# Round-robin PSUM banks for a fast-matrix-product MLP, and attention sums in four column tiles

## The chip, the cores and the metric

One core of a Trainium2 chip. The metric is device time in microseconds (us) of one execution. Ratios are the mean time of one kernel's fast runs over that of the other's fast runs of the same rounds, so they are not quite the ratio of the medians quoted beside them; brackets hold their 95% interval.

TensorE multiplies matrices; VectorE, ScalarE and GpSimd work element by element. A *bank* is one PSUM tile of 128 x 512 fp32, in which a product is summed; the program lets the next product into it only when the readers of the last one are through. A *column tile* is a matmul that uses 64 or 32 of TensorE's 128 columns (a *row tile*, 64 of its rows), so that several can be in flight; the *mode* is how TensorE is divided. In a timeline, brackets at the end of a line hold the engine's idle time before it and what ended it.

## The reference

```python
q, k, v: (8, 12, 448, 64)            # batch, heads, sequence, head_dim, fp32
q_n, k_n = rmsnorm(q, g_q), rmsnorm(k, g_k)
attn = softmax(q_n @ k_n.T / sqrt(64))
x = (attn @ v) as (8*448, 12*64)     # bridge
h = x @ w_in                         # (3584, 768) @ (768, 2048)
out = (h - tanh(h)) @ w_out          # (3584, 2048) @ (2048, 768)
```

## The kernel before: the parts concerned

TensorE runs two streams, interleaved by hand. *Attention* goes in 48 steps, one per batch and pair of heads (six to a batch): scores transposed (keys on partitions), `exp` on ScalarE, sums over keys as a product with ones, values. *MLP* of batch b-1 runs between the pieces of attention of batch b; `run(gap)` issues a quarter of a step's share of it. From batch 1 on, both MLP layers use a seven-product scheme for 2 x 2 blocks: a *set* is seven products, several of which accumulate in the same PSUM bank, and readers combine them.

```python
ORDER = (1, 5, 6, 2, 7, 3, 4)
ps_s = pool("ps_s", bufs=4, space=PSUM)     # attention: four banks
ps_m = pool("ps_m", bufs=1, space=PSUM)     # MLP: "ma", "mc" once, "mb" twice
...
def totals(s, dn):                          # sums over keys: two column tiles of 64
    ...
    nc.tensor.matmul(dn[h * D : (h + 1) * D, :S], lhsT=ones[:CP, :D], rhs=p[:, h, :], ...)
    rd = sp.tile([P, S], F32, name="rd")
    nc.vector.reciprocal(rd, dn[:, :S])
...
def slot(s):                                # one step of attention
    scores(s + 1, 0); load(s + 2, "v")
    run(gap)
    norm(s + 3)                             # GpSimd: squares and a power; VectorE: sums
    rd = totals(s, sc_bank()); divide(s, values(s, sc_bank()), rd)
    run(gap)
    scores(s + 1, 1); add(s + 1)            # VectorE adds four tiles of exponentials to one
    run(gap)
    turn(s + 2, sc_bank(), sc_bank())       # transposes
    norm_q(s + 3); load(s + 4, "kq")
    run(gap)
```

(`has(...)` guards and the loop over products are cut.) After product 3 of a set `shrink` (tanh on ScalarE, a subtraction on GpSimd) and then `factors` (VectorE: a difference that needs that subtraction) are put off to the end of the next product.

## Time and profile before

| | |
|---|---|
| time | 1589.95 us median of 4 (1588.75 to 1591.17) |
| TensorE / VectorE / ScalarE / GpSimd busy | 94 / 50 / 28 / 39% |
| a normal step in steady state | 29.85 us |
| one step in each batch | 31.76 us |

The last two rows come from the starts of the transposes in the trace. The long step looks like this in the timeline of the kernel before (start, length, engine, line, operation):

```profile
995.32 2.43 PE L448 MATMUL ma<-xT,w_f 128*128 128x224 f32 x12
995.36 3.17 DVE L376 TENSOR_TENSOR sum<-sum,p 112x896 f32<-112x896 f32 x2 [1.19 <-ACT p L362]
998.44 0.62 DVE L530 TENSOR_TENSOR s<-mb,s 128x448 f32<-128x448 f32 x1
999.11 1.78 PE L448 MATMUL mb<-xT,w_f 128*128 128x224 f32 x8 [1.36 <-DVE s L530]
```

VectorE adds exponentials until 998.5; only then does it read product 6 out of bank `mb` (L530), and product 7, which accumulates in that bank, starts 1.36 us late.

### The profile page before, as it was taken

What the parts mean: (1) busy time and instruction counts of PE and PEld (TensorE: products, weight loads), DVE (VectorE), ACT (ScalarE), POOL (GpSimd) and SP (SyncE); (2) the same over time, 40 slices, a digit from 0 to 9 for tenths busy, and PEclk for the clock granted to TensorE, in tenths of its full rate; (3) what the DMA queues carried; (4) which work ended last, traced back from release to release, by engine and by line L of the source; (5) the groups of instructions that cost most, each with busy time, mean ns of one, the idle gap of its engine ahead of it and who ended that gap; (6) DMA issues with size and microseconds to landing.
All of it is one profiled execution on the core that took longest, in us unless ns stands there. A gap on an engine that the chain in (4) does not pass through costs nothing.

```text
span 1588.6 us, 19983 instructions
## 1 busy us (share of the span) xinstructions
PE 1494.3 (94%) x7440; PEld 1164.7 (73%) x7440; DVE 788.6 (50%) x1004; ACT 446.4 (28%) x870; POOL 624.4 (39%) x516
## 2 busy tenths in 40 slices
PE   3988768998999999999999999999999999999997
PEld 1336456446878878878877887787877887789997
DVE  6788558865454345434544445434544344522211
ACT  4554234512322223222331232321331232210210
POOL 6655446552452234422453235423444234311410
PEclk9999879999999999999999999999999999999999
DMA  7554575577545554555554564465454664455564
GB/s 193 177 181 165 195 256 166 138 196 229 164 141 161 147 151 144 152 166 148 154 170 123 158 177 131 147 184 139 137 167 133 171 166 137 135 152 162 174 196 105
DMA packets 253983, 257.80 MB, mean 162 GB/s; under 512 B 143413, under 2 KB 198709, under 8 KB 253877
## 3 DMA queue, kind: packets, MB, share of 16 engines
q1 hardware_dynamic: 253552, 256.43, 55.4%
q8 instruction: 61, 1.00, 0.3%
q14 instruction: 46, 0.37, 0.1%
q10 hardware_dynamic: 324, 0.00, 0.0%
HBM read 223.35 MB, written 33.03 MB: 161 GB/s over the span
## 4 chain that ended last, share of the span: by engine, by line
PE 74%; DVE 13%; POOL 3%; DMA 3%; issue 2%; ACT 2%; SPq 2%; ACTq 0%; DVEq 0%; POOLq 0%
PE mb L448 24%; PE ma L448 16%; PE mc L448 15%; PE sc L357 8%; PE sc L383 6%; DVE rd L400 2%; DVE w_out L79 2%; PE sc L395 2%; POOL sq L310 2%; DVE sum L376 2%; DMA w_f<-w_in 1%; PE mb L616 1%; DVE rr L311 1%; ACT p L362 1%; DVE w_out L82 1%
## 5 line engine op out<-in xcount | busy, mean ns | idle before, releaser
L362 ACT ACTIVATE p<-sc,rr 112x448 f32<-112x448 f32 x384 | 212.5, 638 | 224.0 <-PE sc L357 162.0
L448 PE MATMUL mb<-tt,w_f 128*128 128x224 f32 x768 | 166.5, 361 | 17.3 <-DMA w_f<-w_in 16.3
L357 PE MATMUL sc<-qT,kT 64*112 64x448 f32 x768 | 179.5, 574 | 2.2 <-DVE rd L400 1.5
L448 PE MATMUL ma<-xT,w_f 128*128 128x224 f32 x768 | 163.8, 365 | 11.9 <-DMA w_f<-w_in 11.9
L448 PEld LDWEIGHTS mb<-tt,w_f 128*128 128x128 f32 x768 | 142.6, 192 | 42.6 <-issue 22.8
L448 PEld LDWEIGHTS ma<-xT,w_f 128*128 128x128 f32 x768 | 149.7, 197 | 18.7 <-issue 6.2
L315 POOL TENSOR_TENSOR rr<-rr,neg_half 112x16 f32<-112x16 f32 (+1 forms) x49 | 140.7, 2871 | 51.3 <-DVE rr L314 50.3
L400 DVE RECIPROCAL rd<-sc 128x448 f32<-128x448 f32 x42 | 124.0, 2953 | 34.9 <-PE sc L395 34.0
L448 PE MATMUL ma<-gT,w_f 128*128 128x224 f32 x672 | 139.2, 356 | 0.0
L448 PEld LDWEIGHTS ma<-gT,w_f 128*128 128x128 f32 x672 | 125.3, 190 | 15.3 <-issue 15.3
L448 PE MATMUL mb<-tg,w_f 128*128 128x224 f32 x672 | 135.1, 354 | 0.0
L383 PE MATMUL sc<-p,v_nat 112*64 112x448 f32 x672 | 133.4, 539 | 0.0
L448 PEld LDWEIGHTS mb<-tg,w_f 128*128 128x128 f32 x672 | 126.2, 190 | 7.3 <-issue 7.3
L376 DVE TENSOR_TENSOR sum<-sum,p 112x896 f32<-112x896 f32 x80 | 95.8, 1198 | 58.2 <-ACT p L362 52.6
L357 PEld LDWEIGHTS sc<-qT,kT 64*112 64x112 f32 x768 | 65.9, 176 | 79.4 <-issue 62.1
L535 POOL TENSOR_TENSOR u<-u,s 128x448 f32<-128x448 f32 x32 | 36.5, 1141 | 221.0 <-DVE u L534 194.7
L311 DVE TENSOR_REDUCE rr<-sq 112x8 f32<-112x512 f32 x96 | 65.4, 681 | 113.9 <-POOL sq L310 113.9
L310 POOL TENSOR_TENSOR sq<-q_nat 112x512 f32<-112x512 f32 x48 | 50.0, 1041 | 150.5 <-DVE rr L311 103.2
L383 PEld LDWEIGHTS sc<-p,v_nat 112*64 112x64 f32 x672 | 48.3, 137 | 78.0 <-issue 78.0
L448 PE MATMUL mb<-xT,w_f 128*128 128x224 f32 x384 | 87.4, 366 | 17.2 <-DVE s L530 11.4
L504 POOL TENSOR_TENSOR gT<-s,th 128x448 f32<-128x448 f32 x64 | 75.0, 1172 | 62.1 <-ACT th L503 62.1
L448 PEld LDWEIGHTS mb<-xT,w_f 128*128 128x128 f32 x384 | 71.3, 194 | 34.6 <-issue 20.4
(108 smaller groups left out, 2146.0 us busy)
## 6 DMA issues: line engine op xcount, KB each, us to landing
w_f<-w_in SPq DMA_DIRECT2D x224, 384.0 KB, 3.6
w_f<-w_out SPq DMA_DIRECT2D x147, 512.0 KB, 4.3
w_raw<-in_moe_w_out_dram SPq DMA_DIRECT2D x32, 384.0 KB, 3.4
k_nat<-in_k_dram SPq DMA_DIRECT2D x96, 112.0 KB, 3.3
q_nat<-in_q_dram SPq DMA_DIRECT2D x48, 224.0 KB, 3.7
v_nat<-in_v_dram SPq DMA_DIRECT2D x48, 224.0 KB, 4.7
w_in<-w_out SPq DMA_DIRECT2D x28, 384.0 KB, 5.6
out_dram<-th SPq DMA_DIRECT2D x192, 56.0 KB, 2.7
```

The costliest lines, as they stand in the source:

```text
L79: nc.vector.tensor_scalar(out=bits, in0=bits, scalar1=4, scalar2=1, op0=ALU.logical_shift_left, op1=ALU.logical_shift_right)
L310: nc.gpsimd.tensor_tensor(out=sq, in0=rows, in1=rows, op=ALU.mult)
L311: nc.vector.reduce_sum(rr[:, "kq".index(name)], sq, axis=AX.X)
L315: nc.gpsimd.tensor_tensor(out=r, in0=r, in1=neg_half[:, : r.shape[1]], op=ALU.pow)
L357: nc.tensor.matmul(sc[:CP, :S], lhsT=kT[r, c * CP : (c + 1) * CP], rhs=qT[r, :], start=True, stop=True)
L362: nc.scalar.activation(p[:, h, i, :], tiles[h][:CP, :S], AF.Exp, scale=rr[:, 0, 2 * c + h : 2 * c + h + 1])
L376: nc.vector.tensor_tensor(out=t, in0=t, in1=part, op=ALU.add)
L383: nc.tensor.matmul(av[h * D : (h + 1) * D, :S], lhsT=v_nat[:, h, c, :], rhs=p[:, h, c % 2, :], start=(c == 0), stop=(c == NCH - 1),)
L400: nc.vector.reciprocal(rd, dn[:, :S])
L448: nc.tensor.matmul(bank[:, f * HS : (f + 1) * HS], lhsT=w[:, f * depth + c, :], rhs=moving[p](c), start=(first and f == 0 and c == 0), sto ...
L504: eng.tensor_tensor(out=g[:, rows, cols], in0=h, in1=th, op=ALU.subtract)
L535: nc.gpsimd.tensor_tensor(out=u3, in0=u3, in1=s5, op=ALU.add)
```

## The change

Its intent: give every MLP bank more time between two products, halve TensorE's time for the sums over keys, and leave MLP's tiling mode twice in a step rather than three times.

```diff
-    ORDER = (1, 5, 6, 2, 7, 3, 4)
+    ORDER = (1, 5, 6, 2, 3, 7, 4)
-    ps_s = pool("ps_s", bufs=4, space=PSUM)
-    ps_m = pool("ps_m", bufs=1, space=PSUM)
+    ps_s = pool("ps_s", bufs=5, space=PSUM)
+    ps_m = pool("ps_m", bufs=3, space=PSUM)
...
+            for p in ORDER:
+                first = p not in (2, 3, 7)
+                bank = banks[p] = mm_bank() if first else banks[{2: 1, 3: 5, 7: 6}[p]]
...                                       # readers of products 5 and 7 (layer 1; layer 2 likewise)
-                    nc.scalar.copy(out=s5, in_=v)
+                    nc.vector.tensor_tensor(out=s5, in0=v, in1=s1, op=ALU.add)
...
-                    nc.vector.tensor_tensor(out=u3, in0=v, in1=s1, op=ALU.add)
-                    nc.gpsimd.tensor_tensor(out=u3, in0=u3, in1=s5, op=ALU.add)
+                    nc.vector.tensor_tensor(out=u3, in0=v, in1=s5, op=ALU.add)
+                    nc.vector.tensor_tensor(out=s1, in0=v, in1=s1, op=ALU.add)
...
+    def totals_by_halves(s, dn):         # four column tiles: 2 heads x 2 halves of the queries
+        ...
+                    r = (2 * h + n) * BL
+                    nc.tensor.matmul(dn[r : r + BL, :HS], lhsT=ones[:CP, :BL],
+                                     rhs=p[:, h, n * HS : (n + 1) * HS], ...)
+        nc.vector.reciprocal(rs, dn[:, :HS])
...                                       # rows_out: 4 rows to DRAM; rows_in: back to 128 partitions
+    def late_slot(s):                    # from batch 2 on, in place of slot
+        totals_by_halves(s, sc_bank()); scores(s + 1, 0); load(s + 2, "v")
+        run(gap / 2)
+        rows_out(s); norm(s + 3)
+        run(gap / 2)
+        rows_in(s); turn(s + 2, sc_bank(), sc_bank()); load(s + 4, "kq")
+        run(gap)
+        divide(s, values(s, sc_bank())); scores(s + 1, 1); add(s + 1)
+        run(gap)
+        norm_q(s + 3)
+        run(gap)
```

(Cut: guards, layer 2, and the rest of `factors`, which is split by product.)

More of the change, by code (lines that the diff above doesn't have):

```diff
@@ L143, in bounded_path, with mm_bank @@
     wp = wp_stack.enter_context(tc.tile_pool(name="wp", bufs=1))
-    ps_s = pool("ps_s", bufs=4, space=PSUM)
-    ps_m = pool("ps_m", bufs=1, space=PSUM)
-    def mm_bank(tag):
-        return ps_m.tile([P, 512], F32, name=tag, bufs=2 if tag == "mb" else 1)
+    ps_s = pool("ps_s", bufs=5, space=PSUM)
+    ps_m = pool("ps_m", bufs=3, space=PSUM)
+    def mm_bank():
+        return ps_m.tile([P, 512], F32, name="mm")
     loaded = {}
@@ L298, in ring_load @@
                 nc.sync.dma_start(out=t, in_=w_out_dram[:, BLOCKS[p], j].rearrange("p f d -> p (f d)"))
-    normed, turned, probs, sums, xT, tt = {}, {}, {}, {}, {}, {}
+    normed, turned, probs, sums, whole, xT, tt = {}, {}, {}, {}, {}, {}, {}
     def norm(s):
@@ L398, in totals, with rows_out, rows_in, divide @@
                 )
-        rd = sp.tile([P, S], F32, name="rd")
+        rd = whole[s] = sp.tile([P, S], F32, name="rd")
         nc.vector.reciprocal(rd, dn[:, :S])
-        return rd
-    def divide(s, av, rd):
+    def totals_by_halves(s, dn):
+        t = sums.pop(s)
+        parts = t if t else [probs[s, c // 2][:, :, c % 2, :] for c in range(NCH)]
+        for i, p in enumerate(parts):
+            for h in range(2):
+                for n in range(2):
+                    r = (2 * h + n) * BL
+                    nc.tensor.matmul(
+                        dn[r : r + BL, :HS], lhsT=ones[:CP, :BL], rhs=p[:, h, n * HS : (n + 1) * HS],
+                        start=(i == 0), stop=(i == len(parts) - 1),
+                    )
+        rs = whole[s] = sp.tile([P, HS], F32, name="rs")
+        nc.vector.reciprocal(rs, dn[:, :HS])
+    def rows_out(s):
+        rs = whole[s]
+        row = whole[s] = scratch.tile([2, S], F32, name="row", bufs=2)
+        nc.sync.dma_start(
+            out=row.rearrange("h (n q) -> (h n) q", n=2), in_=rs.rearrange("(g i) q -> g i q", i=BL)[:, 0, :]
+        )
+    def rows_in(s):
+        row = whole[s]
+        rd = whole[s] = sp.tile([P, S], F32, name="rd")
+        nc.sync.dma_start(
+            out=rd,
+            in_=bass.AP(tensor=row.tensor, offset=row.offset, ap=[[S, 2], [0, D], [1, S]]),
+        )
+    def divide(s, av):
         b, hp = steps[s]
+        rd = whole.pop(s)
         x = xT[b, hp] = xp.tile([P, S], F32, name="xT")
@@ L439, in products @@
         took = 4 * HS / ENGINE_NS
+        banks = {}
         def product(j, p, bank, first):
@@ L458, in product @@
                 fn()
-        pending = None
         for j in range(count):
             use = done_with(j)
-            ma, mc = mm_bank("ma"), mm_bank("mc")
-            yield from product(j, 1, ma, True)
-            use(1, ma)
-            yield took
-            if pending:
-                yield from pending()
-            yield from product(j, 5, mc, True)
-            use(5, mc)
-            yield took
-            mb = mm_bank("mb")
-            yield from product(j, 6, mb, True)
-            use(6, mb)
-            yield took
-            for p, bank in ((2, ma), (7, mb), (3, mc)):
-                yield from product(j, p, bank, False)
+            for p in ORDER:
+                first = p not in (2, 3, 7)
+                bank = banks[p] = mm_bank() if first else banks[{2: 1, 3: 5, 7: 6}[p]]
+                yield from product(j, p, bank, first)
                 use(p, bank)
                 yield took
-            def pending(j=j, mb=mb, use=use):
-                yield from product(j, 4, mb, False)
-                use(4, mb)
-                yield took
-        yield from pending()
     def hidden(b):
@@ L508, in done_with, with factors @@
             s1, s2, s5, u3 = part("s1"), part("s2"), part("s5"), part("u3")
-            def factors(first):
+            def factors(p):
                 if b == 0:
@@ L515, in factors @@
                 f1, f2, f4 = (t2[:, i, up] for i in range(3))
-                if first:
+                if p == 3:
                     nc.vector.tensor_tensor(out=f1, in0=g12, in1=g11, op=ALU.subtract)
+                elif p == 7:
                     nc.vector.tensor_tensor(out=f2, in0=g22, in1=f1, op=ALU.subtract)
@@ L533, in use, with rest @@
                 elif p == 7:
-                    nc.vector.tensor_tensor(out=u3, in0=v, in1=s1, op=ALU.add)
-                    nc.gpsimd.tensor_tensor(out=u3, in0=u3, in1=s5, op=ALU.add)
-                    late["todo"].append(lambda: shrink(down, high, u3, nc.gpsimd))
+                    nc.vector.tensor_tensor(out=u3, in0=v, in1=s5, op=ALU.add)
+                    nc.vector.tensor_tensor(out=s1, in0=v, in1=s1, op=ALU.add)
+                    def rest():
+                        shrink(down, high, u3, nc.gpsimd)
+                        factors(7)
+                    late["todo"].append(rest)
                 elif p == 3:
@@ L541, in rest @@
                         shrink(up, high, s2, nc.gpsimd)
-                        factors(True)
+                        factors(3)
                     late["todo"].append(rest)
@@ L549, in rest @@
                         shrink(down, low, s1, nc.gpsimd)
-                        factors(False)
+                        factors(4)
                     late["todo"].append(rest)
@@ L584, in use @@
                 elif p == 5:
-                    nc.scalar.copy(out=s5[:, low], in_=v)
+                    nc.vector.tensor_tensor(out=s5[:, low], in0=v, in1=s1[:, low], op=ALU.add)
                 elif p == 6:
@@ L590, in use @@
                 elif p == 7:
-                    nc.vector.tensor_tensor(out=y2[:, high], in0=v, in1=s1[:, low], op=ALU.add)
-                    nc.gpsimd.tensor_tensor(out=y2[:, high], in0=y2[:, high], in1=s5[:, low], op=ALU.add)
+                    nc.vector.tensor_tensor(out=y2[:, high], in0=v, in1=s5[:, low], op=ALU.add)
+                    nc.vector.tensor_tensor(out=s1[:, low], in0=v, in1=s1[:, low], op=ALU.add)
                 elif p == 3:
@@ L611, in project_first @@
         for n in range(CD):
-            bank = mm_bank("mb")
+            bank = mm_bank()
             for f in range(CF):
@@ L667, in first_slot @@
         if has(s + 2):
-            turn(s + 2, mm_bank("mb"), mm_bank("mb"))
+            turn(s + 2, mm_bank(), sc_bank())
         load(s + 4, "kq")
@@ L674, in first_slot @@
         if has(s):
-            rd = totals(s, mm_bank("mc"))
+            totals(s, mm_bank())
         if has(s + 2):
@@ L682, in first_slot @@
         if has(s):
-            divide(s, values(s, mm_bank("ma" if s < NP - 1 else "mb")), rd)
+            divide(s, values(s, mm_bank()))
         if has(s + 3):
@@ L696, in slot @@
             norm(s + 3)
-        rd = totals(s, sc_bank())
-        divide(s, values(s, sc_bank()), rd)
+        totals(s, sc_bank())
+        divide(s, values(s, sc_bank()))
         run(gap)
@@ L710, in slot @@
         run(gap)
+    def late_slot(s):
+        gap = gap_ns(s)
+        totals_by_halves(s, sc_bank())
+        if has(s + 1):
+            scores(s + 1, 0)
+        if has(s + 2):
+            load(s + 2, "v")
+        run(gap / 2)
+        rows_out(s)
+        if has(s + 3):
+            norm(s + 3)
+        run(gap / 2)
+        rows_in(s)
+        if has(s + 2):
+            turn(s + 2, sc_bank(), sc_bank())
+        if has(s + 4):
+            load(s + 4, "kq")
+        run(gap)
+        divide(s, values(s, sc_bank()))
+        if has(s + 1):
+            scores(s + 1, 1)
+            add(s + 1)
+        run(gap)
+        if has(s + 3):
+            norm_q(s + 3)
+        run(gap)
     load(0, "kq")
@@ L718, in bounded_path @@
     for s in range(NP, NS):
-        slot(s)
+        slot(s) if s < 2 * NP else late_slot(s)
     run(1e9)
```

## The prediction

> **What bounds the kernel now.** I read the page first (busy shares, slices, clock), then the table of windows by stage, then the waits of TensorE, then the timeline of one attention step, which is the unit that repeats.
>
> The page says that TensorE is busy for nearly the whole span at full clock, and that the idle part lies in the first quarter:
>
> ```profile
> PE 1494.3 (94%) x7440; PEld 1164.7 (73%) x7440; DVE 788.6 (50%) x1004; ACT 446.4 (28%) x870; POOL 624.4 (39%) x516
> ...
> PE   3988768998999999999999999999999999999997
> ...
> PEclk9999879999999999999999999999999999999999
> ...
> L448 PE MATMUL mb<-tt,w_f 128*128 128x224 f32 x768 | 166.5, 361 | 17.3 <-DMA w_f<-w_in 16.3
> ...
> L395 PE MATMUL sc<-sum,ones 112*64 112x448 f32 x160 | 38.9, 565 | 0.0
> ```
>
> Three windows, chosen by stage (weights still being converted; steady; MLP alone), give the same in numbers:
>
> ```profile
> 115.00:265.00 150.00, 113.83 (x515) 85.32 (x512) 106.91 (x148) 59.14 (x120) 73.91 (x58) 0.87 0.62 202
> 409.00:1406.00 997.00, 988.88 (x5149) 802.76 (x5148) 455.37 (x547) 266.91 (x514) 376.11 (x314) 1.00 0.52 152
> 1433.00:1580.00 147.00, 147.00 (x777) 144.25 (x776) 32.18 (x53) 17.18 (x35) 33.32 (x31) 1.00 0.58 166
> ```
>
> The columns are the window, its length, then PE, PEld, DVE, ACT and POOL busy, clock, DMA share and GB/s. In the middle 997 us TensorE is idle for 8.1 us and VectorE busy for under half: TensorE's own work sets the time there, and only fewer TensorE cycles or the removal of those 8.1 us can shorten it. From 115 to 265 us it is idle for 36 us; another chain sets the time there.
>
> The waits of TensorE over the whole run name both kinds of idleness:
>
> ```profile
> PE mb L337 <- DVE n L321: 25.9, 6, 7.6
> PE mb L448 <- DMA w_f<-w_in: 22.1, 3, 11.0
> PE ma L448 <- DMA w_f<-w_in: 11.9, 4, 4.6
> PE mb L448 <- DVE s L530: 11.4, 7, 3.3
> ```
>
> The first lies before 115 us (the first queries are normalised late), the next two are weight blocks that come late in batch 0, and the fourth is the one that recurs: 8.1 us of it are six waits of 1.36 us, one per batch, and 3.3 us one wait in batch 0.
>
> One attention step in steady state, TensorE alone (start, length, then the group):
>
> ```profile
> 915.43 1.76 PE L357 MATMUL sc<-qT,kT 64*112 64x448 f32 x8
> 917.12 2.54 PE L448 MATMUL ma<-xT,w_f 128*128 128x224 f32 x12
> 919.50 2.43 PE L448 MATMUL mc<-tt,w_f 128*128 128x224 f32 x12
> 921.77 0.92 PE L448 MATMUL mb<-tt,w_f 128*128 128x224 f32 x4
> 922.62 0.97 PE L395 MATMUL sc<-sum,ones 112*64 112x448 f32 x4
> 923.42 3.18 PE L383 MATMUL sc<-p,v_nat 112*64 112x448 f32 x16
> 926.53 1.78 PE L448 MATMUL mb<-tt,w_f 128*128 128x224 f32 x8
> ```
>
> Lengths overlap, so I take starts. One matmul of the program is two records. From 919.50 to 921.77 twelve MLP records take 2.27 us, 189 ns each. The sums over keys (L395) hold TensorE from 922.62 to 923.42, 0.80 us for two head halves side by side. Read instruction by instruction, two such records start 6 to 8 ns apart and the next two 376 ns later (448 columns), except the first round, 426 ns. From one start of L395 (922.62) to the next (952.47) a step is 29.85 us; one step in each batch is 31.76.
>
> **What the Trainium skill says.** "TensorEngine Tiling (Array Packing)", section Key Properties: changing the tiling mode drains TensorE, and tiles run independently. The trace agrees: the last MLP record before the sums starts 283 ns ahead of them where 189 is normal (+94), the first round costs another 50, and the way back costs 95 and 104 more.
>
> "TensorE: Matmul & The Clock Gate", section Part 3: Packing small matmuls, gives a pack's span as one matmul plus about 4 ns for each further tile. The 6 to 8 ns between the two tiles here agree; that four column tiles in fp32 do the same, no trace here shows yet.
>
> The same page, section Architectural detail, calls ScalarE and VectorE strict FIFO. The recurring wait is this: the add that frees a product's bank (L530) stands behind the sums of attention, which wait for exponentials, and came at 998.44 for a product finished about a microsecond earlier.
>
> "DMA: Bandwidth & Descriptors", Anatomy of one DMA, gives a fixed cost of about 2.0 us plus bytes over 436 GB/s. This trace lands 56 KB in 2.7 us and 224 KB in 3.7 to 4.7 us, so the same size of cost.
>
> **The change part by part.**
>
> 1. *Sums over keys in four column tiles, from batch 2 on (36 of 48 steps).* Four tiles of 32 columns by 224 queries replace two of 64 by 448. A round of 224 fp32 columns should take half of 376, 188 ns, and there are still two rounds: 752 becomes 376 ns, if the four tiles really run at once. Saved: 0.376 us a step.
>
> 2. *Fewer trips away from MLP mode.* Before, a step has three trips into a tiled mode: scores, sums with values, scores. Measured over the steady stage as the time from the last MLP start before to the second after, less two times 189 ns: scores 1.889 us against 4 x 0.376 = 1.504 pure, so 0.385 of switching; sums and values 4.107 against 3.760, so 0.347. In all 2 x 0.385 + 0.347 = 1.117 us. After, there are two: sums with scores, values with scores. Each has an entry (0.144), an exit (0.200) and an inner change, which batch 0's prologue shows for values to scores as 94 + 91 = 0.185 us. That is 2 x 0.529 = 1.058. Saved: 0.059. Parts 1 and 2: 0.43 us a step, x 36 = 15.5 us. The transposes move but run in MLP's mode.
>
> 3. *MLP banks go round.* Before, product 7 accumulates on 6's bank with only product 2 between, so 6's reader has one product (2.27 us) before TensorE waits. After, in order 1, 5, 6, 2, 3, 7, 4, every second product on a bank, and every reuse of a bank, has two products between (4.5 us). L530's delay of 1.36 us fits in. The step that holds it is 1.9 us long over the normal one (31.76 - 29.85; scores stretched by a late bank are in it, and attention's fifth bank should end them). Saved: 6 x 1.9 = 11.4 us steady, and 3.3 us in batch 0.
>
> 4. *Readers of the banks.* Product 5's copy (ACT, 521 ns) becomes a VectorE add, product 7 gets a second VectorE add, and GpSimd's add (1141 ns) goes. VectorE gets 2 x 0.62 us more in each of four sets and 2 x 0.39 in each of three projections: 7.3 us a batch. Against it the reciprocal (2953 ns for 448 columns) works on 224, by proportion 1.48 us: six steps give 8.9 us back. VectorE stays at half busy, off the path.
>
> 5. *Rows through DRAM.* The reciprocals go out as 4 rows and come back to 128 partitions (229 KB). From the steps above: sums end at about T+0.6 us, reciprocal T+2.3, out issued then and landed near T+5, back near T+9. The multiplication that needs it follows values at about T+17 (sums and scores 2.4, two MLP gaps of 5.2, transposes 0.8, values 3.1). So hidden, with 8 us to spare. The load adds 36 x 0.23 = 8 MB to 257.
>
> 6. *Batch 0.* Product 4 now runs before the next set's product 1, so one weight block is fetched ahead of the seven writes that keep a set in DRAM. In the before trace block 6 of the second set waited 10.98 us behind these. I expect TensorE to have one product (2.3 us) more done when it stalls, but VectorE's conversion now also stands behind product 5, which ACT served before. Net 1 us saved, give or take 5.
>
> Sum: 15.5 + 11.4 + 3.3 + 1 = 31 us. I take off 4 us for new waits: the multiplication, then the sums' adds, now come in one burst after values, and VectorE is blocked there for about 5 us. So 1590.4 - 27 = 1563 us.
>
> **The rivals.**
>
> A. *Four tiles don't overlap, or pay per instruction.* Sixteen matmul and weight records fall in 0.38 us, 24 ns each; the transposes here issue eight in 0.385 us, 48 ns each, but those are bound by their 112 columns. If 48 ns were the limit, the sums would take 0.8 us again and part 1 would give nothing: 1576. The queue running ahead of TensorE speaks against it.
>
> B. *The wait moves.* The burst on VectorE delays some other reader by more than two products, or sums at the head of a step wait for the adds. The adds should end about 8 us after values start and the sums come 15 us after: little room for it. If once per batch 1.5 us come back: 1572.
>
> C. *Broadcast late.* If the DMA queue stands still for over 8 us, values' multiplication waits; TensorE would feel it only through the fifth bank. In 36 steps of 1 us: 1595 or more. The steady queue keeps five blocks ahead, which speaks against it.
>
> D. *Batch 0 gains more.* The 36 us idle there is latency in a loop, and taking GpSimd's add out of it could give 5 to 10 us: 1555.
>
> **Range and chances.** The steady part is well determined (15 and 11 us, each give or take 3), batch 0 is not (give or take 5), and new waits can only cost. 8 in 10: 1552 to 1577. The 2% line is 1558.6, half a standard deviation below my figure: faster 0.30, within 2% 0.69, slower 0.01.
>
> **What would show it.** The step in steady state 29.4 us, all six of a batch alike; sums from first start to the scores' start about 0.53 us with the mode change (0.42 without); no wait of TensorE for the product 6 add; the reciprocal at 1.5 us; the broadcast landed before values end; idle from 115 to 265 us still near 30 us. I am wrong if four tiles start more than 20 ns apart, if a step still stays at 29.8, if a new VectorE or DMA wait of TensorE over 5 us in sum appears after 400 us, or if batch 0 moves by more than 6 us.

## The result, and the profile after

1572.99 us, median of 4 (1571.13 to 1575.12), against 1589.95: ratio 0.9894 [0.9877, 0.9911], within 2% and inside the range, 10 us above the figure. From the page and from a table of windows of the changed kernel:

```profile
PE 1474.9 (94%) x7584; PEld 1159.5 (74%) x7584; DVE 771.3 (49%) x1110; ACT 424.8 (27%) x817; POOL 615.0 (39%) x463
```

```profile
115.00:265.00 150.00, 117.84 (x520) 88.00 (x520) 107.52 (x159) 59.02 (x120) 71.69 (x57) 0.89 0.64 209
400.00:1390.00 990.00, 980.37 (x5316) 805.68 (x5315) 437.29 (x628) 253.74 (x480) 379.91 (x276) 1.00 0.56 161
```

TensorE is still the bound, with 32 us idle in the early window and 9.6 us in the steady one (36 and 8.1 before). The steady idle time is not gone. From 400 to 1400 us it has one new name (total, times, longest):

```profile
PE mm L481 <- issue: 9.6, 6, 1.6
```

One step of the changed kernel, TensorE alone:

```profile
933.27 0.59 PE L411 MATMUL sc<-sum,ones 112*32 112x224 f32 x8
933.78 1.76 PE L358 MATMUL sc<-qT,kT 64*112 64x448 f32 x8
...
940.88 0.55 PE L334 MATMUL sc<-ident,k_nat 112*128 112x112 f32 x4
...
947.05 3.23 PE L384 MATMUL sc<-p,v_nat 112*64 112x448 f32 x16
950.21 1.76 PE L358 MATMUL sc<-qT,kT 64*112 64x448 f32 x8
```

The sums hold TensorE from 933.27 to 933.78, 0.51 us with the mode change that follows (0.80 before, where values follow in the same mode). Read one by one, the four tiles start 6 to 8 ns apart and the second round 214 ns after the first: they do run at once. A normal step is 29.42 us, 0.43 less than before.

But one step in each batch takes 31.52 us. Here it is, one stretch on TensorE, VectorE, ScalarE and GpSimd:

```profile
966.67 0.58 ACT L517 ACTIVATE th<-s 128x448 f32<-128x448 f32 x1 [0.22 <-DVE s L558]
967.25 1.04 POOL L311 TENSOR_TENSOR sq<-q_nat 112x512 f32<-112x512 f32 x1 [9.33 <-DVE rr L312]
...
968.03 2.43 PE L481 MATMUL mm<-tt,w_f 128*128 128x224 f32 x12
...
969.30 2.90 POOL L316 TENSOR_TENSOR rr<-rr,neg_half 112x16 f32<-112x16 f32 x1 [1.01 <-DVE rr L315]
...
971.07 2.45 PE L481 MATMUL mm<-xT,w_f 128*128 128x224 f32 x12
972.16 1.13 POOL L518 TENSOR_TENSOR gT<-s,th 128x448 f32<-128x448 f32 x1
...
973.33 0.62 DVE L531 TENSOR_TENSOR tg<-gT 128x448 f32<-128x448 f32 x1 [4.11 <-POOL gT L518]
973.87 0.62 DVE L549 TENSOR_TENSOR u<-mm,s 128x448 f32<-128x448 f32 x1
974.41 0.62 DVE L550 TENSOR_TENSOR s<-mm,s 128x448 f32<-128x448 f32 x1
...
975.12 1.19 PE L481 MATMUL mm<-tt,w_f 128*128 128x224 f32 x5 [1.61 <-issue]
```

Read it backwards. TensorE wants the bank of product 7 for the next set's product 5. Product 7's two adds (L549, L550) end at 975.02; the product itself was done at about 968.2, just after product 4 began to run (968.03). They stand behind L531, a difference that needs GpSimd's subtraction L518, and L518 stands behind the normalisation's power L316, 2.90 us. The column says "issue", so the profile shows nothing that TensorE waited for; that it was this bank is read from the VectorE rows (the adds end 0.10 us before product 5 starts), and late_factors and four_four test it. Start by start, product 5 makes 1.85 us of the long step's 2.10; the other 0.26 falls on product 6, which starts at 977.62 when product 4's add, behind the same queue, has left its bank (977.57).

Where the 19.4 us between the two profiled runs (1588.6 and 1569.2) went, by milestones of the MLP stream in the traces:

| stretch | before | after | difference |
|---|---|---|---|
| start to batch 0's MLP | 120.4 | 119.2 | -1.2 |
| batch 0's MLP | 245.9 | 240.3 | -5.6 |
| batch 1, layer 1 | 98.9 | 101.0 | +2.1 |
| from there to the last batch | 987.9 | 974.2 | -13.7 |
| last batch | 135.5 | 134.5 | -1.0 |

### The profile page after: what moved, and what is told of

It is laid out like the page before. It is cut to its first block, busy times and chain, and to the rows that moved or that the text cites. A ratio compares the mean times of both kernels' runs of the same rounds, so it can differ in the third digit from the quotient of the medians.

```text
span 1569.2 us, 20495 instructions
## 1 busy us (share of the span) xinstructions
PE 1474.9 (94%) x7584; PEld 1159.5 (74%) x7584; DVE 771.3 (49%) x1110; ACT 424.8 (27%) x817; POOL 615.0 (39%) x463
## 4 chain that ended last, share of the span: by engine, by line
PE 85%; DVE 5%; issue 3%; DMA 2%; POOL 2%; SPq 1%; ACT 1%; ACTq 0%; POOLq 0%; DVEq 0%
PE mm L481 60%; PE sc L358 9%; PE sc L384 8%; PE mm L636 4%; DMA w_f<-w_in 1%; PE sc L411 1%; PE sc L338 1%; DVE w_out L79 1%; DVE rd L401 1%; PE sc L334 1%; POOL sq L311 1%; SPq L262 1%; DVE rr L312 1%; POOL gT L518 1%; PE mm L396 1%
## 5 line engine op out<-in xcount | busy, mean ns | idle before, releaser
L481 PE MATMUL mm<-xT,w_f 128*128 128x224 f32 x1536 | 318.2, 363 | 31.0 <-DMA w_f<-w_in 25.3
L481 PEld LDWEIGHTS mm<-xT,w_f 128*128 128x128 f32 x1536 | 294.3, 195 | 54.7 <-issue 39.6
L481 PEld LDWEIGHTS mm<-gT,w_f 128*128 128x128 f32 x1344 | 251.4, 190 | 23.7 <-issue 14.0
L481 PE MATMUL mm<-gT,w_f 128*128 128x224 f32 x1344 | 267.8, 355 | 0.0
L481 PE MATMUL mm<-tt,w_f 128*128 128x224 f32 x1152 | 240.9, 360 | 18.8 <-issue 9.6
L481 PEld LDWEIGHTS mm<-tt,w_f 128*128 128x128 f32 x1152 | 218.1, 193 | 35.8 <-issue 27.3
L481 PE MATMUL mm<-tg,w_f 128*128 128x224 f32 x1008 | 200.4, 353 | 0.0
L481 PEld LDWEIGHTS mm<-tg,w_f 128*128 128x128 f32 x1008 | 189.5, 190 | 0.0
L518 POOL TENSOR_TENSOR gT<-s,th 128x448 f32<-128x448 f32 x64 | 78.2, 1222 | 229.5 <-ACT th L517 229.0
L316 POOL TENSOR_TENSOR rr<-rr,neg_half 112x16 f32<-112x16 f32 (+1 forms) x49 | 140.2, 2862 | 51.6 <-DVE rr L315 50.6
L90 POOL TENSOR_TENSOR w_out<-w_out,w_raw 128x384 int32<-128x384 int32 x44 | 47.8, 1087 | 84.0 <-DVE w_out L82 43.1
L636 PE MATMUL mm<-gT,w_out 128*128 128x448 f32 x192 | 75.4, 545 | 1.4 <-POOL w_out L90 1.4
```

Of the source, the lines that this page charges most:

```text
L90: nc.gpsimd.tensor_tensor(out=bits, in0=bits, in1=raw[:, :, 0], op=ALU.add)
L316: nc.gpsimd.tensor_tensor(out=r, in0=r, in1=neg_half[:, : r.shape[1]], op=ALU.pow)
L481: nc.tensor.matmul(bank[:, f * HS : (f + 1) * HS], lhsT=w[:, f * depth + c, :], rhs=moving[p](c), start=(first and f == 0 and c == 0), sto ...
L518: eng.tensor_tensor(out=g[:, rows, cols], in0=h, in1=th, op=ALU.subtract)
L636: nc.tensor.matmul(bank[:, :S], lhsT=w_out_sb[f][:, n * P : (n + 1) * P], rhs=g[:, f, :], start=(f == 0), stop=(f == CF - 1),)
```

## The experiments

In the diffs, "changed" is the changed kernel. Times are medians of 4; the kernel before ran beside each at 1590.4 to 1590.5 us.

| run | us | ratio to before | normal step | long step |
|---|---|---|---|---|
| changed (for reference) | 1573.0 | 0.9894 | 29.42 | 31.52 |
| tiles_only | 1612.5 | 1.0140 [1.0121, 1.0159] | 30.79 | none |
| banks_only | 1576.8 | 0.9914 [0.9896, 0.9933] | 29.85 | none |
| two_tiles | 1589.5 | 0.9997 [0.9975, 1.0020] | 29.81 | 32.09 |
| late_factors | 1565.9 | 0.9841 [0.9820, 0.9863] | 29.42 | 30.09 |
| norm_moved | 1561.7 | 0.9817 [0.9801, 0.9834] | 29.42 | none |
| late_norm | 1561.0 | 0.9814 [0.9798, 0.9831] | 29.42 | none |
| cheap_pow (wrong) | 1553.0 | 0.9763 [0.9747, 0.9780] | 29.42 | none |
| four_four | 1607.9 | 1.0117 [1.0099, 1.0134] | 30.78 | none |
| norm_early | 1574.9 | 0.9896 [0.9875, 0.9917] | 29.85 | none |

### The new step alone: tiles_only

```diff
 # kernel before, plus from the change:
+ totals_by_halves, rows_out, rows_in, late_slot; late_slot from batch 2 on
 # MLP's banks, order and readers, and attention's four banks, as before
```

> Before's MLP banks and order, with the new attention step alone (four column tiles, rows through DRAM, two trips), so attention has four PSUM banks. Theory 1 (the step saving is independent of the banks): 36 x 0.43 = 15.5 us off, about 1574 us, step 29.42 us. Theory 2 (the fifth bank is needed): the last of the four score tiles takes the bank of values and waits for the multiplication, an estimated 0.4 to 0.6 us a step, 14 to 21 us in all, which eats the saving: 1588 to 1596 us, step 29.8 to 30.0, with TensorE waiting for the multiplication in every step.

Measured: 1.4% longer (within the 2% line, but clear of 1), a step of 30.79 us, worse than either theory. The sums with scores take 3.373 us over MLP's own pace where the changed kernel takes 2.405, values with scores 5.425 against 5.046. The second of these, 0.38 us, is the wait that I had foreseen; the first, 0.97 us, I had missed. In the trace of tiles_only:

```profile
896.32 0.58 PE L410 MATMUL sc<-sum,ones 112*32 112x224 f32 x8
896.84 2.79 PE L357 MATMUL sc<-qT,kT 64*112 64x448 f32 x8
896.98 1.56 DVE L415 RECIPROCAL rs<-sc 128x224 f32<-128x224 f32 x1 [2.44 <-PE sc L410]
```

The four score tiles take 2.79 us where 1.76 is normal. Sums and four score tiles need five banks; with four, the last score tile takes the sums' bank, and that is read until the reciprocal ends at 898.54 (the tile's first record starts at 898.63). The Trainium skill has the principle in "TensorEngine Tiling (Array Packing)", section PSUM Bottleneck: tiling speeds up TensorE but not the emptying of PSUM. The trace agrees: the sums now take 0.5 us, the reader of their bank 1.56. So the fifth bank is no refinement: the column tiles and the two trips are a loss of 22 us without it.

### The banks alone: banks_only

```diff
-        slot(s) if s < 2 * NP else late_slot(s)
+        slot(s)
```

> The changed kernel with the old attention step throughout (two column tiles, no DRAM). Theory 1 (the banks remove the product 6 wait and nothing replaces it): 1590 - 11.4 - 3.3 = 1575 us, all six steps of a batch at 29.85. Theory 2 (the wait moves to another reader on VectorE, as the trace of the changed kernel suggests): one step in six stays 1.5 to 2 us longer and only batch 0 gains, about 5 us: 1583 to 1587 us.

Theory 1 held in the steady part. All steps take 29.85 us, and TensorE has no wait at all from 400 to 1400 us. The time, 1576.8, is 2 us above theory 1's figure. The banks alone thus give most of what the whole change gives, and the wait that replaced L530's in the changed kernel is not a property of the new banks by themselves.

### Two tiles in the new step: two_tiles

```diff
-        totals_by_halves(s, sc_bank())
+        totals(s, sc_bank())
-        rows_out(s)
-        rows_in(s)
```

> The changed kernel with its new order of the step, but sums in two tiles of 64 columns by 448 and the reciprocal of all rows on chip, nothing through DRAM. If the four tiles run at once, each step is 0.376 us longer: 29.80 us, 13.5 us in all, 1586 us (the reciprocal of 2.95 us in place of 1.56 may add up to 1.4 us once per batch). If the trip through DRAM costs time that the trace does not show, or four tiles give nothing, it stays near 1573 us. The order of the step alone, against before, should then be worth only 0.06 us a step.

A step is 29.81 us, 0.39 longer than with four tiles; sums with scores take 2.791 us over MLP's pace against 2.405; values with scores (5.046) and transposes (0.785) are unchanged. This is the price of the two tiles, as expected, and 29.85 to 29.81 is that of the order of the trips. The whole time is 16.5 us above the changed kernel's; the long step's share of that is 6 x 0.2 (its excess is 2.28 us against 2.10). The trip through DRAM costs nothing that this pair could show, though tiles and trip were changed together.

### The difference after the adds: late_factors

```diff
                     def rest():                      # after product 3
                         shrink(up, high, s2, nc.gpsimd)
-                        factors(3)
...
                     def rest():                      # after product 7
                         shrink(down, high, u3, nc.gpsimd)
+                        factors(3)
                         factors(7)
```

> The changed kernel with the first difference that VectorE takes after product 3 (factors(3)) issued one product later, behind product 7's two adds. If the new wait once per batch comes from those adds standing behind that difference, which waits for GpSimd, it goes: six steps alike at 29.42 us, 6 x 2.1 = 12.6 us off, 1560 us. If the wait is TensorE's own or comes from elsewhere, the long step stays at 31.5 us and the time near 1573 us.

The long step shrank from 31.52 to 30.09 us: 6 x 1.43 = 8.6 us, and the medians differ by 7.1. So the adds behind L531 were most of the wait; the 12.6 us hoped for did not all come. A rest stays, 0.67 us a long step, and the waits from 400 to 1400 us have one line:

```profile
PE mm L481 <- DVE s L566: 2.4, 6, 0.4
```

L566 is product 4's add. The difference still waits for GpSimd, and now product 4's reader stands behind it instead of product 7's.

### The normalisation half a gap later: norm_moved, late_norm

```diff
         rows_out(s)
-        if has(s + 3):
-            norm(s + 3)
         run(gap / 2)
         rows_in(s)
+        if has(s + 3):
+            norm(s + 3)
```

late_norm is this together with late_factors.

> The changed kernel with the normalisation of a later step issued half an MLP gap later (2.6 us), nothing else. Theory 1 (the long step is GpSimd's power, issued just ahead of product 3's subtraction, then VectorE's difference and product 7's adds behind it): six steps alike at 29.42 us or nearly so, up to 12.6 us off, 1560 to 1565 us. Theory 2 (the wait is due to VectorE's burst after values, as the prediction had it): the long step stays, 1573 us.

> Both mends together: the difference after product 7's adds, and the normalisation half a gap later. Under theory 1 no wait of TensorE is left in steady state: 29.42 us for all steps, 1560 us, and 4 us under the run with the difference alone (long step 30.08). Under theory 2 as that run, 1566 us.

The long step is gone: all steps are 29.42 us, and the time falls to 1561.7 us. In the trace of norm_moved:

```profile
964.60 1.13 POOL L518 TENSOR_TENSOR gT<-s,th 128x448 f32<-128x448 f32 x1 [9.59 <-ACT th L517]
...
965.77 0.63 DVE L531 TENSOR_TENSOR tg<-gT 128x448 f32<-128x448 f32 x1 [1.92 <-POOL gT L518]
966.31 0.62 DVE L549 TENSOR_TENSOR u<-mm,s 128x448 f32<-128x448 f32 x1
966.85 0.62 DVE L550 TENSOR_TENSOR s<-mm,s 128x448 f32<-128x448 f32 x1
...
974.32 2.90 POOL L316 TENSOR_TENSOR rr<-rr,neg_half 112x16 f32<-112x16 f32 x1 [1.01 <-DVE rr L315]
```

The subtraction now starts as soon as its tanh is there, and the power comes ten microseconds later. late_norm adds nothing that the intervals tell apart from norm_moved (0.9814 and 0.9817), and there was no wait left in the steady part for it to take. Both are faster than the changed kernel, by 11 to 12 us, and than the one before; norm_moved is the simpler version to keep.

### A cheap power: cheap_pow

```diff
-            nc.gpsimd.tensor_tensor(out=r, in0=r, in1=neg_half[...], op=ALU.pow)
+            nc.gpsimd.tensor_scalar(out=r, in0=r, scalar1=-0.5, scalar2=1.5, op0=ALU.mult, op1=ALU.add)
```

> The changed kernel with GpSimd's power (2.9 us for 112 x 16) replaced by one multiply-add there (1.5 - 0.5 r, right only near 1, so a result wrong on purpose by some per cent), a fraction of a microsecond. Under theory 1 the long step shrinks from 31.52 to 29.42 or at most 29.9 us: 10 to 12.6 us off, and up to 10 us more from the prologue, where queries wait for the same power: 1550 to 1563 us. Under theory 2 the long step stays at 31.5 us.

The result is wrong (relative error 0.16). The steady part is the point: six equal steps of 29.42 us with the normalisation at its place in the changed kernel. The power's 2.90 us is what makes the long step. Batch 0's MLP starts at 111.5 us, 7.7 earlier than in the changed kernel, which accounts for the rest of the gain: the prologue waits for the same power.

### Four banks each: four_four

```diff
-    ps_s = pool("ps_s", bufs=5, space=PSUM)
-    ps_m = pool("ps_m", bufs=3, space=PSUM)
+    ps_s = pool("ps_s", bufs=4, space=PSUM)
+    ps_m = pool("ps_m", bufs=4, space=PSUM)
```

> The changed kernel with four banks for MLP and four for attention instead of three and five. If the step with two trips needs the fifth bank whatever MLP does, as the run of the new step alone showed (0.97 us lost in sums with scores, 0.38 in values with scores), each step is 30.8 us: 1573 + 36 x 1.35 = 1622 us less up to 12 us if the long step hides in it. If MLP's old banks were what made that run slow, it stays at 1573 us.

A step is 30.78 us, and the two bursts take 3.373 and 5.425 us, as in tiles_only. The loss of that run comes from attention's missing bank, whatever MLP does with its own. The long step is gone too: 1573 + 36 x 1.36 - 12.6 = 1609, measured 1607.9. It does not hide in the stretched steps, though, as the expectation had it: the fourth MLP bank removes it. From a timeline of four_four from 993 to 996 us, in the step where it would stand:

```profile
993.92 2.24 PE L481 MATMUL mm<-tt,w_f 128*128 128x224 f32 x11
...
994.98 0.61 DVE L550 TENSOR_TENSOR s<-mm,s 128x448 f32<-128x448 f32 x1
```

Product 7's adds are as late as in the changed kernel (they end 6.99 us after product 4's start in both), yet product 5 starts 1.67 us before they end. With four banks in turn it takes the bank of product 3, not that of product 7. That shows which bank TensorE waited for in the changed kernel.

### The early normalisation in the old step: norm_early

```diff
 # banks_only, from batch 2 on:
-        run(gap)
-        norm(s + 3)
+        run(gap / 2)
+        norm(s + 3)
+        run(gap / 2)
         totals(s, sc_bank())
```

> The new banks with the old attention step (six equal steps of 29.85 us, 1576.8 us), with one difference: from batch 2 on the normalisation is issued half an MLP gap (2.6 us) earlier, where the changed kernel has it. If the place of the normalisation alone makes the long step, it appears here too, without column tiles and without the trip through DRAM: one step in six 31 to 32 us, 6 x 1.6 to 2.1 = 10 to 13 us more, 1587 to 1590 us. If the long step needs the new attention step (its burst on VectorE, its reciprocals, its DMAs), all steps stay at 29.85 and the time at 1577 us.

A miss for the theory that the place alone does it: all steps stay at 29.85 us. The trace of norm_early shows why:

```profile
968.79 2.43 PE L481 MATMUL mm<-tt,w_f 128*128 128x224 f32 x12
...
970.07 2.90 POOL L316 TENSOR_TENSOR rr<-rr,neg_half 112x16 f32<-112x16 f32 x1 [1.01 <-DVE rr L315]
971.15 0.97 PE L396 MATMUL sc<-sum,ones 112*64 112x448 f32 x4
971.96 3.18 PE L384 MATMUL sc<-p,v_nat 112*64 112x448 f32 x16
...
972.93 1.14 POOL L518 TENSOR_TENSOR gT<-s,th 128x448 f32<-128x448 f32 x1
...
974.65 0.62 DVE L549 TENSOR_TENSOR u<-mm,s 128x448 f32<-128x448 f32 x1
...
977.44 1.30 PE L481 MATMUL mm<-tt,w_f 128*128 128x224 f32 x6
```

Product 7's adds are just as late as in the changed kernel (5.84 us after product 4's start there, 973.87 - 968.03, and 5.86 here, 974.65 - 968.79). But the old step has sums and values, 3.9 us of TensorE, between product 4 and the next set's products, and TensorE asks for the bank only at 977.44, after the adds. The new step has only the transposes there, 0.77 us. With banks_only and norm_moved this makes a table of two by two, all with three MLP banks: the long step exists only where the normalisation comes early *and* sums and values have moved away.

## Why the prediction was right or wrong

It fell in its range and chose the right class. The time came out 10 us above its figure, 17 us gained rather than 27. Term by term:

**Four column tiles and fewer trips (15.5 us).** Right. A step fell from 29.85 to 29.42 us, and the bursts measure 2.405 and 5.046 us over MLP's pace, where the working gives 0.529 + 1.880 = 2.409 and 0.529 + 4.512 = 5.041. The split is right too: two_tiles gives 0.39 to the tiles and 0.04 to the order. Rival A, that the tiles pay per instruction, is out.

**Banks go round (11.4 us steady, 3.3 in batch 0).** Right by itself, as banks_only shows: no wait remains in the steady part, and the run is 13.6 us faster than the kernel before where the terms say 14.7. One reading behind the term was wrong: L530 did not come for "a product finished about a microsecond earlier". Product 6's last record starts at 995.13 and ends by about 995.5, so L530, at 998.44, was 3 us late and TensorE felt 1.36 of them. The 4.5 us that two products give covered that as well. In the changed kernel nothing of the 11.4 us is left, because 6 x 2.1 = 12.6 us came back.

**New waits (4 us taken off).** This is the step that failed: "I take off 4 us for new waits: the multiplication, then the sums' adds, now come in one burst after values, and VectorE is blocked there for about 5 us." The size was 12.6 us, and the place was another one. No wait of TensorE from 400 to 1400 us came from the burst after values. Two of the prediction's own signs of being wrong showed it: one step in six is not like the others, and a new wait sums to 9.6 us where it had set 5 as the limit. The part-by-part list left out one move that stands in the diff: `norm` comes half a gap earlier, which puts its power in front of product 3's subtraction in one step of each batch. The rule that saved L530, two products between a product and the next use of its bank, allowed for 4.5 us; product 7's first add came 5.8 us after product 4 had begun, and part 2 had moved the sums and values whose TensorE time would have covered it. Rival B named the outcome ("If once per batch 1.5 us come back: 1572") but looked to VectorE's burst for the cause; that its 1572 is so near 1573.0 is in part luck.

**Strict order.** The Trainium skill's word that VectorE is strict FIFO ("TensorE: Matmul & The Clock Gate", section Architectural detail) explained the wait before. The same section says the like of GpSimd ("per-Q7 strict FIFO"), and the trace agrees: L518, ready at about 967.3 (its tanh ran from 966.67 for 0.58 us), started at 972.16, behind the squares and the power; between these two GpSimd stood idle for 1.01 us and did not take it. The prediction applied the rule to one queue where two in a row were at work.

**Batch 0 (3.3 + 1 us).** Right in size; which of its two terms gave it was not tried. From the start of batch 0's MLP to batch 1's, the eight correct kernels with the new banks average 242.3 us (240.3 to 243.5), the two with the old banks 245.9 and 247.0: 4.2 us. Of the changed kernel some of it is given back at once: its wait for batch 1's first weight blocks is 7.8 us against 4.6, and it is 5.1 to 8.5 in the other kernels with the new banks. (The prediction counts the 4.6 us in batch 0; it is at 382.05 us, in batch 1's first set.) The stretch from batch 1's start to the end of that wait is 15.8 us before and 15.7 after: it holds sums and values (3.9 us) before and only transposes (0.8 us) after, so the longer wait is about the attention work that left. Why the blocks come no earlier was not tried; it stays open.

**Rows through DRAM (hidden).** Right. In the step shown the row goes out at 935.53 and the broadcast is issued at 937.69, after the row has landed; the multiplication runs at 950.33, after values. VectorE waits for the broadcast in two of 36 steps, and TensorE in none. Rival C did not happen.

**VectorE's load.** Right in sign: its busy time fell by 17 us over the run (the working, 8.9 less 7.3 us a batch, gives about 10), and the reciprocal of half the columns takes 1554 ns, near the 1.48 us by proportion. "Off the path" did not hold: one step in six waited for VectorE's queue.

With the measured sizes the sum is 15.5 - (12.6 - 11.4) + 4.2 = 18.5 us, against 17.0 in the timed runs and 19.4 in the profiled one, which was the fastest of the four.

## What to carry to other kernels

When work moves within a hand-made schedule, list every operation that changes its place, the small ones of engines off the critical path too: a 2.9 us GpSimd operation moved by 2.6 us cost 11 to 12 us of time here. The reach of a bank is counted from its reader's whole queue, through every engine that the queue waits for, and the TensorE work that happens to lie between is part of the slack; take it away and a delay that was always there begins to cost. And before two changes are judged apart, see whether one pays for the other: the column tiles lost 22 us without the fifth bank that the MLP's rearrangement set free.

## What the Trainium skill lacked or had wrong

- "TensorEngine Tiling (Array Packing)", Key Properties, says that a change of mode drains TensorE but not what that costs. Here, beyond the time of the matmuls themselves: 144 ns into two column tiles (120 into four), 185 to 205 ns from column tiles to row tiles, 200 ns back to the full array.
- "TensorE: Matmul & The Clock Gate", Part 3, gives about 4 ns for each further tile. In fp32, with 112 rows, four column tiles started 6 to 8 ns apart, and the second round of 224 columns came 214 ns after the first.
- The same page gives no case of column tiles whose bank has a slow reader (the tiling page has the principle, no figure). Here a 0.5 us product held its bank for 1.56 us more, and with one bank too few that cost 0.97 us a step.
- No page that I read has a duration for GpSimd's elementwise power. Here 112 x 16 elements took 2.92 us in the mean of the kernel before (112 x 8: 1.67 us), over twice a subtraction of 128 x 448 (1.17 us).
- No page that I read has a duration for VectorE's reciprocal: 2.95 us for 448 fp32 columns and 1.55 us for 224.
